# Linear attention and a gated block on one core: unit 0's key exponentials read from the projections' banks, in a new order of operations

## The chip, the core and the metric

The kernel runs on one NeuronCore of a Trainium2 chip. The core's engines work in parallel, each through its own instructions in program order: PE (TensorE, matrix products), DVE (VectorE), ACT (ScalarE, exponentials and copies), POOL (GpSimd) and SP (SyncE, which here only issues transfers). The metric is the device time of one execution in microseconds (us), less is better.

## The reference

Queries, keys and values have 8 batches, 8 heads, 576 tokens and 64 columns. Each of queries and keys is projected onto 128 features, the largest absolute value of a token's projection is subtracted, and the exponential is taken of it and of its negative:

```python
def phi(x):
    proj = np.einsum('bhsd,df->bhsf', x, w_phi)
    proj = proj - np.max(np.abs(proj), axis=-1, keepdims=True)
    return np.concatenate([np.exp(proj), np.exp(-proj)], axis=-1)
q_p, k_p = (phi(q), phi(k))
kv = np.einsum('bhsf,bhsd->bhfd', k_p, v)
z = np.sum(k_p, axis=2)
num = np.einsum('bhsf,bhfd->bhsd', q_p, kv)
den = np.einsum('bhsf,bhf->bhs', q_p, z)[..., None] + 1e-06
```

The quotient num / den, laid out as 4608 tokens of 512 columns, goes through a second block: `h = x @ w_in` (1024 columns), a row's softmax times h, a normalisation over the row, and `@ w_out` back to 512 columns.

## The kernel before

The attention is cut into 16 units (u = 0 to 15) of half a batch, four heads each, and a unit into two subs of two heads. The 576 tokens of a sub's two pairs are taken in groups g = 0, 1, 2 (`GROUPS`): groups 0 and 2 are four tiles of 128 tokens, group 1 is the one tile that the two subs share. The second block has 36 tiles of 128 tokens ("moe", t).

Every piece of work is an `op` with a name, an engine and what it must follow, and the tuple `SEQUENCE`, written out by a search, fixes the order in which the 2458 ops are issued. Each engine runs its own ops in just that order, SP its transfers too. Buffers are rings of slots by tag, handed out in the same order; PSUM has six single banks ("a") and one pair ("h").

The ops that matter here, by name and by the tiles that the profile shows:

- `kp`/`qp` (PE, `pjk`, `pjq`): the projections of a group's keys or queries, both heads of a pair, into two banks, 16 profile records each. `pm` (`pjm`) is that of group 1.
- `km`/`qm` (DVE, `m`): the largest absolute value of each token; `ks`/`qs` (DVE, `dk`, `dq`): projection minus that maximum.
- `ke` (ACT, `ek<-dk`): the exponentials of a key block, first of `dk`, then of its negative, 128x512 each. `qx` (ACT, `fq`) is the same of queries, after a transposition (`dT` on PE for units 0 and 1, through DRAM for the others).
- `K`, `rest`, `Z` (PE, `kvT`): the products with the values and the sums z. For units 3 and up z is added up on POOL first (`zt`, `zacc`). From unit 2 on `kve` (DVE, `kvs`) turns kvT in blocks, `kvo` (SP, `dk<-kvs`) writes it to DRAM and `kvi` (SP, `kvf<-dk`) brings it back as `kvf`.
- `qo`, `qr`, `qd` (PE, `num`, `kvT<-fq,kvf`, `den`): the numerator and the denominator, which read `kvf`. `dv` (POOL, `xa`, `xb`) multiplies by the reciprocal, broadcast back by transfers (`rb`).
- moe `xh`, `xl` (the row block split into two parts, `mxh`, `mxl`), `h` (PE), `mx`, `ex`, `u` (softmax weights), `tb`, `bo`, `bi` (a turn through DRAM, `ub`, `du`, `uTs`), `uh`, `ul`, `o` (PE), `oe` (ACT, `os<-o,sc`) and `od` (SP, `out<-os`). The last tile, 35, is done in two halves of 256 columns (`moe_o_last`).

For units in `K_BANKED` the plan replaces `ks` and `ke` of groups 0 and 2; the tuple is empty before:

```python
if u in K_BANKED:
    add(("kn", g, j), "gpsimd", 250, zj + 0.3, k_neg, (g, j), [("km", g, j)], [("m", ("kn", g, j))], [("m", g, j)])
else:
    add(("ks", g, j), "vector", dve(512), zj + 0.3, k_sub, (g, j), [("km", g, j)], [("d", ("d", g, j))], pj + [("m", g, j)])
```

Of the kernel before, what the change touches and what calls it, by code (L numbers as in the profile page):

```python
# [32 lines left out]
K_BANKED = ()  # L33
# [22 lines left out]
    2, 123, 1, 124, 125, 78, 127, 126, 313, 94, 87, 85, 129, 80, 81, 95, 128, 82, 83, 99, 96, 84, 98, 136, 97,  # L56
    135, 101, 102, 138, 141, 103, 142, 104, 10, 79, 89, 130, 90, 314, 100, 92, 91, 131, 105, 86, 173, 224, 88,
    218, 4, 133, 112, 315, 132, 134, 317, 106, 107, 113, 114, 139, 108, 174, 93, 175, 11, 115, 219, 137, 316,
    110, 12, 178, 116, 109, 111, 117, 143, 222, 189, 181, 180, 182, 33, 140, 5, 118, 154, 13, 179, 318, 220,
    176, 6, 199, 119, 157, 145, 14, 120, 121, 221, 223, 156, 155, 148, 160, 190, 15, 149, 177, 162, 159, 184,  # L60
    28, 38, 150, 284, 22, 275, 122, 158, 161, 197, 34, 200, 183, 198, 191, 194, 192, 187, 193, 7, 195, 201, 225,
    164, 185, 144, 202, 167, 146, 35, 186, 226, 188, 196, 8, 227, 228, 39, 163, 205, 206, 29, 165, 147, 166,
    203, 207, 43, 285, 168, 422, 36, 3, 169, 289, 40, 286, 30, 23, 208, 288, 41, 287, 209, 249, 31, 290, 230,
    204, 213, 214, 232, 233, 236, 231, 255, 44, 381, 252, 210, 268, 151, 372, 235, 215, 234, 296, 24, 229, 291,
    251, 211, 45, 9, 46, 276, 25, 216, 212, 270, 423, 152, 254, 217, 237, 238, 32, 37, 271, 250, 240, 273, 424,
    272, 278, 153, 243, 274, 416, 277, 239, 256, 257, 253, 269, 170, 171, 244, 426, 16, 425, 259, 258, 319, 245,
    241, 42, 292, 262, 48, 49, 365, 246, 172, 279, 297, 50, 325, 427, 263, 260, 449, 242, 294, 382, 47, 264,
    320, 261, 280, 386, 417, 295, 293, 247, 326, 26, 281, 282, 265, 17, 266, 418, 283, 485, 469, 520, 51, 476,
    450, 27, 248, 419, 383, 302, 327, 420, 52, 300, 18, 303, 388, 385, 384, 323, 19, 298, 299, 53, 304, 367,
    321, 301, 267, 368, 305, 421, 369, 387, 308, 20, 21, 1808, 309, 389, 306, 374, 307, 1844, 332, 1826, 334,  # L70
    1809, 521, 72, 322, 324, 486, 329, 60, 328, 1810, 1811, 66, 63, 373, 375, 390, 330, 393, 333, 331, 69, 67,
    522, 345, 428, 370, 310, 371, 593, 336, 394, 61, 524, 1845, 68, 523, 490, 1812, 335, 339, 492, 525, 1813,
    1814, 346, 429, 399, 75, 628, 376, 379, 340, 377, 62, 337, 338, 391, 584, 347, 471, 311, 366, 378, 474, 487,
    73, 1846, 312, 392, 348, 76, 349, 351, 352, 395, 472, 341, 430, 634, 451, 350, 380, 1847, 488, 1817, 491,
    489, 353, 64, 70, 397, 1848, 405, 355, 400, 57, 401, 71, 354, 65, 1827, 54, 1849, 398, 432, 1862, 357, 396,
    55, 532, 1850, 1853, 586, 533, 406, 434, 356, 407, 408, 1828, 1829, 435, 342, 470, 585, 433, 58, 359, 358,
    437, 497, 436, 409, 1854, 475, 410, 1815, 1851, 1830, 74, 431, 473, 493, 455, 498, 594, 629, 411, 439, 438,
    630, 595, 631, 598, 478, 1855, 597, 632, 494, 596, 600, 633, 402, 403, 56, 1831, 404, 412, 360, 599, 413,
    1832, 59, 503, 77, 440, 443, 457, 456, 452, 343, 534, 361, 1818, 1856, 495, 1863, 453, 539, 635, 536, 480,
    362, 363, 414, 496, 1864, 1857, 444, 344, 504, 1852, 477, 1835, 481, 577, 479, 415, 364, 505, 1865, 538,  # L80
    441, 1858, 640, 636, 1866, 483, 482, 1867, 537, 454, 1868, 1859, 509, 459, 1860, 1819, 499, 500, 442, 458,
    637, 638, 484, 1833, 510, 511, 460, 445, 526, 1871, 639, 1820, 698, 579, 512, 461, 540, 501, 506, 1821,
    1816, 535, 446, 690, 541, 462, 463, 502, 464, 580, 447, 705, 1861, 513, 527, 1822, 582, 1872, 1823, 465,
    528, 641, 448, 514, 515, 587, 466, 530, 1869, 529, 1870, 531, 507, 553, 467, 740, 554, 696, 508, 581, 583,
    605, 601, 602, 543, 542, 516, 1824, 606, 544, 611, 588, 468, 545, 517, 665, 1873, 518, 547, 603, 546, 1880,
    604, 741, 742, 697, 555, 589, 548, 744, 556, 1881, 706, 612, 591, 707, 613, 578, 746, 519, 1836, 590, 743,
    1882, 1883, 607, 558, 557, 559, 561, 549, 710, 745, 708, 712, 592, 709, 1884, 560, 562, 700, 566, 666, 703,
    563, 617, 564, 1885, 567, 618, 1886, 565, 569, 568, 619, 642, 817, 689, 550, 1837, 1898, 609, 1934, 610,
    608, 647, 852, 1874, 1935, 1875, 1834, 648, 649, 701, 1936, 620, 1887, 752, 571, 570, 1937, 1876, 1952, 702,
    621, 753, 711, 622, 704, 572, 1938, 1889, 1939, 644, 646, 721, 717, 718, 645, 1899, 1940, 691, 853, 856,  # L90
    650, 643, 614, 1877, 615, 722, 652, 616, 667, 551, 854, 1941, 552, 671, 1900, 1901, 653, 573, 692, 1943,
    1838, 694, 651, 855, 1902, 655, 574, 754, 654, 623, 858, 1878, 1903, 857, 693, 695, 1904, 624, 1953, 1839,
    719, 656, 747, 801, 808, 1890, 575, 668, 657, 713, 714, 625, 669, 803, 659, 748, 658, 1907, 672, 720, 715,
    716, 670, 806, 626, 818, 749, 804, 750, 660, 1825, 802, 627, 822, 819, 674, 821, 1954, 673, 1840, 1888,
    1942, 723, 576, 726, 727, 724, 725, 676, 824, 864, 820, 675, 805, 1841, 661, 1842, 677, 751, 729, 807, 823,
    825, 679, 826, 678, 756, 730, 964, 680, 1891, 731, 732, 827, 681, 683, 759, 761, 1892, 865, 662, 921, 1908,
    699, 663, 757, 810, 929, 733, 760, 859, 1909, 682, 1916, 860, 777, 684, 862, 1905, 965, 861, 758, 1910,
    1893, 1955, 1894, 829, 830, 828, 685, 734, 778, 1895, 920, 735, 686, 767, 762, 1956, 863, 966, 968, 763,
    728, 664, 835, 967, 969, 687, 1944, 809, 755, 1957, 1896, 766, 764, 930, 1958, 769, 812, 765, 1959, 1961,
    889, 815, 1897, 813, 1879, 779, 736, 768, 688, 1988, 780, 783, 2024, 782, 785, 771, 1041, 1843, 737, 1989,  # L100
    1911, 1962, 1026, 1990, 1991, 816, 931, 1960, 2025, 836, 738, 1992, 1993, 1912, 772, 1994, 1997, 814, 890,
    739, 1963, 932, 2006, 781, 1913, 2026, 2027, 841, 784, 934, 1970, 790, 791, 970, 1906, 1082, 1032, 1998,
    770, 773, 866, 774, 811, 831, 786, 1964, 913, 832, 788, 837, 936, 787, 1965, 935, 1914, 1995, 2028, 789,
    933, 842, 2007, 792, 843, 838, 2029, 871, 941, 793, 844, 833, 971, 873, 891, 834, 795, 2030, 868, 794, 915,
    839, 2008, 895, 1945, 2009, 1999, 896, 845, 942, 892, 870, 893, 869, 1966, 796, 840, 916, 976, 972, 2010,
    2033, 974, 918, 917, 973, 2011, 1917, 867, 1971, 1076, 1033, 922, 775, 846, 797, 1915, 874, 1967, 2034, 872,
    776, 924, 876, 919, 923, 798, 977, 878, 879, 847, 975, 2012, 877, 1001, 875, 881, 848, 937, 1968, 938, 927,
    880, 1077, 925, 928, 939, 883, 2000, 894, 940, 897, 947, 1042, 1972, 849, 1080, 1043, 850, 1078, 2001, 1996,
    1079, 945, 884, 2013, 1002, 914, 851, 978, 885, 1003, 2015, 1973, 948, 2002, 1025, 1046, 1045, 898, 900,
    1946, 946, 980, 882, 2003, 953, 1044, 799, 949, 1974, 902, 903, 1047, 1975, 1081, 926, 899, 1048, 901, 800,  # L110
    1947, 954, 955, 904, 1976, 982, 981, 2004, 905, 907, 1979, 1027, 886, 1188, 1083, 956, 2031, 957, 1086, 943,
    887, 906, 2035, 1028, 1088, 908, 983, 944, 985, 1084, 1030, 958, 1144, 1031, 1194, 1153, 888, 979, 1948,
    909, 1007, 1004, 1918, 1949, 1919, 984, 986, 2036, 987, 1029, 1085, 1087, 2005, 1980, 1089, 1034, 1008, 910,
    1950, 911, 991, 950, 951, 988, 1137, 1090, 990, 952, 2032, 1920, 989, 959, 1113, 1005, 1051, 992, 960, 1052,
    993, 1921, 961, 1922, 995, 912, 994, 2096, 1189, 1154, 1049, 1009, 1036, 1155, 1095, 1190, 1925, 1191, 2097,
    1114, 1923, 2078, 1192, 996, 2098, 2037, 1158, 1039, 962, 1147, 1926, 1156, 1159, 2099, 2038, 1053, 963,
    1146, 1969, 1927, 997, 2016, 1300, 1951, 1115, 998, 2039, 2100, 1050, 1165, 1006, 1097, 1010, 1193, 1065,
    1040, 2014, 1157, 1037, 1014, 2101, 1015, 1057, 1160, 1012, 1054, 2017, 2042, 1058, 1091, 1059, 1060, 2040,
# [1188 lines left out]
```

## Time and profile before

| | |
|---|---|
| median of 3 runs | 663.16 us (662.53 to 663.62) |
| the profiled execution's own time | 664.01 us |
| its span, first to last instruction | 662.2 us |
| PE busy | 653.7 us, 99% of the span |
| DVE, ACT, POOL busy | 495.1, 368.9, 409.1 us |
| granted TensorE clock | 1.000 throughout |

The span leaves out 1.81 us that lie around it in the execution's time. "Busy" is the time in which an engine had an instruction in work; consecutive matmuls overlap, so a busy PE need not run at its best pace.

### The profile page before, as it was taken

What the parts mean: (1) busy time and instruction counts of PE and PEld (TensorE: products, weight loads), DVE (VectorE), ACT (ScalarE), POOL (GpSimd) and SP (SyncE); (2) the same over time, 40 slices, a digit from 0 to 9 for tenths busy, and PEclk for the clock granted to TensorE, in tenths of its full rate; (3) what the DMA queues carried; (4) which work ended last, traced back from release to release, by engine and by line L of the source; (5) the groups of instructions that cost most, each with busy time, mean ns of one, the idle gap of its engine ahead of it and who ended that gap; (6) DMA issues with size and microseconds to landing.
All of it is one profiled execution on the core that took longest, in us unless ns stands there. A gap on an engine that the chain in (4) does not pass through costs nothing.

```text
span 662.2 us, 13124 instructions
## 1 busy us (share of the span) xinstructions
PE 653.7 (99%) x4900; PEld 490.5 (74%) x4900; DVE 495.1 (75%) x750; ACT 368.9 (56%) x713; POOL 409.1 (62%) x447
## 2 busy tenths in 40 slices
PE   8999999999999999999999999999999999999997
PEld 6766767668777777777777777877677877788886
DVE  6999987788978687799968879788679665355340
ACT  4997775466564744556565665355745464324221
POOL 0239998757866546667876575856654775455342
PEclk9999999999999999999999999999999999999999
DMA  8987787887487946887667856874786544424241
GB/s 269 346 270 237 221 251 210 270 259 214 134 265 255 296 151 182 272 260 230 201 197 230 287 151 176 266 227 124 229 282 199 191 149 120 123 110 162 112 167 72
DMA packets 133296, 138.45 MB, mean 209 GB/s; under 512 B 55664, under 2 KB 106736, under 8 KB 132720
## 3 DMA queue, kind: packets, MB, share of 16 engines
q1 hardware_dynamic: 133232, 137.61, 65.9%
q8 instruction: 39, 0.64, 0.4%
q14 instruction: 25, 0.20, 0.1%
HBM read 87.10 MB, written 50.48 MB: 208 GB/s over the span
## 4 chain that ended last, share of the span: by engine, by line
PE 87%; DVE 6%; DMA 4%; issue 1%; ACT 1%; SPq 0%; ACTq 0%
PE o L260 30%; PE h L260 29%; PE kvT L260 11%; PE num L260 6%; PE pjk L260 4%; PE pjq L260 4%; PE den L260 2%; DVE m L260 2%; DVE w L260 1%; DVE dq L260 1%; DMA rawq<-in_q 1%; DVE dk L260 1%; DMA pT<-dqd 1%; PE pjm L260 1%; DMA dk<-kvs 1%
## 5 line engine op out<-in xcount | busy, mean ns | idle before, releaser
L260 POOL TENSOR_TENSOR uls<-uTs,uhs 128x1024 fp32r<-128x1024 f32 x36 | 86.6, 2410 | 61.8 <-ACT uhs L260 47.6
L260 PE MATMUL o<-w_out_h,uhs 128*128 128x512 f32 (+1 forms) x296 | 114.6, 387 | 0.0
L260 ACT ACTIVATE ek<-dk 128x512 f32<-128x512 f32 (+1 forms) x160 | 89.7, 584 | 44.1 <-DVE dk L260 39.4
L260 PE MATMUL o<-w_out_l,uhs 128*128 128x512 f32 (+1 forms) x296 | 113.6, 384 | 0.0
L260 PE MATMUL o<-w_out_h,uls 128*128 128x512 f32 (+1 forms) x296 | 113.5, 383 | 0.0
L260 PE MATMUL h<-win_h,mxh 128*128 128x512 f32 x288 | 91.2, 398 | 0.3 <-DVE dq L260 0.3
L260 DVE TENSOR_REDUCE nm<-h 128x1 f32<-128x1024 f32 x36 | 43.9, 1218 | 62.9 <-PE h L260 62.9
L260 PE MATMUL h<-win_l,mxh 128*128 128x512 f32 x288 | 88.9, 390 | 0.0
L260 PE MATMUL h<-win_h,mxl 128*128 128x512 f32 x288 | 88.8, 389 | 0.0
L260 ACT ACTIVATE fq<-pT 128x512 f32<-128x512 f32 (+1 forms) x140 | 74.5, 559 | 21.4 <-DMA pT<-dqd 13.8
L260 POOL TENSOR_TENSOR zt<-ek 128x512 f32<-128x512 f32 x52 | 68.8, 1322 | 24.4 <-ACT ek L260 22.8
L260 ACT ACTIVATE eu<-h,nm 128x1024 f32<-128x1024 f32 x36 | 40.0, 1111 | 69.3 <-DVE nm L260 60.3
L260 PEld LDWEIGHTS o<-w_out_h,uhs 128*128 128x128 f32 x296 | 55.6, 188 | 13.4 <-issue 1.6
L260 PEld LDWEIGHTS o<-w_out_h,uls 128*128 128x128 f32 x296 | 55.6, 188 | 11.0
L260 PEld LDWEIGHTS o<-w_out_l,uhs 128*128 128x128 f32 x296 | 55.6, 188 | 10.6
L260 PEld LDWEIGHTS h<-win_h,mxh 128*128 128x128 f32 x288 | 52.4, 188 | 13.9 <-issue 1.1
L260 PEld LDWEIGHTS h<-win_l,mxh 128*128 128x128 f32 x288 | 54.0, 188 | 11.5
L260 PEld LDWEIGHTS h<-win_h,mxl 128*128 128x128 f32 x288 | 54.1, 188 | 11.5
L260 PE MATMUL kvT<-ek,rawv 128*64 128x256 f32 x512 | 61.9, 384 | 0.0
L260 POOL TENSOR_TENSOR xa<-E,rb 128x576 f32<-128x576 f32 (+1 forms) x32 | 29.7, 931 | 51.9 <-DMA rb<-d 40.7
L260 DVE TENSOR_TENSOR eu<-h,eu 128x1024 f32<-128x1024 f32 x36 | 43.6, 1212 | 17.9 <-ACT eu L260 17.7
L260 PE MATMUL num<-fq,kvf 128*64 128x448 f32 (+1 forms) x304 | 56.2, 500 | 0.0
(96 smaller groups left out, 1231.9 us busy)
## 6 DMA issues: line engine op xcount, KB each, us to landing
du<-ub SPq DMA_DIRECT2D x36, 512.0 KB, 3.7
uTs<-du SPq DMA_DIRECT2D x36, 512.0 KB, 4.9
rb<-d SPq DMA_DIRECT2D x64, 144.0 KB, 4.4
dqd<-dq SPq DMA_DIRECT2D x14, 640.0 KB, 4.3
pT<-dqd SPq DMA_DIRECT2D x14, 640.0 KB, 5.8
out<-os SPq DMA_DIRECT2D x35, 256.0 KB, 3.2
rawq<-in_q SPq DMA_DIRECT2D x32, 256.0 KB, 4.7
rawk<-in_k SPq DMA_DIRECT2D x32, 256.0 KB, 4.5
```

The lines of the kernel that those rows point to most:

```text
L260: return self.tc.keep_in_program_order(method(*args, **kwargs))
```

## The change

Unit 0's eight key exponentials of groups 0 and 2 (two groups, two heads, two signs) no longer read DVE's differences `dk`. ACT reads the projection straight from its PSUM banks, with the maximum as a bias for each token. A bias is one value for each partition, and a 128x512 block holds four tiles of tokens, so that each exponential is issued as four of 128x128. The negative of the maximum is made by POOL (`kn`). The four `ks` of unit 0 go. These functions stood in the kernel unused:

```python
def k_neg(st, g, j):
    st["kn", g, j] = sb("m", [P, 4], name="kn")
    nc.gpsimd.tensor_scalar(out=st["kn", g, j], in0=st["m", g, j], scalar1=-1.0, scalar2=None, op0=ALU.mult)

def k_exp_banks(st, g, j, s, tag):
    if s == 0:
        st["kf", g, j] = sb(tag, [P, 4, 2, F], name="ek")
    for t in range(4):
        nc.scalar.activation(
            out=st["kf", g, j][:, t, s, :], in_=tokens(st["pj", g][j])[:, t], func=AF.Exp, scale=1.0 - 2.0 * s,
            bias=st["m" if s else "kn", g, j][:, t : t + 1],
        )
```

The diff is one line, and a new `SEQUENCE` for the whole program:

```diff
-K_BANKED = ()
+K_BANKED = (0,)
@@
 SEQUENCE = (
-    2, 123, 1, 124, 125, 78, 127, 126, 313, 94, 87, 85, 129, 80, 81, 95, 128, 82, 83, 99, 96, 84, 98, 136, 97,
...
```

The three places that follow show the new order. The first is ACT at the program's start, before; `ek` are key exponentials, `fq` query exponentials, `wraw` the weights' conversion, `kvs` the copy of unit 0's first kvT.

```order
L260 ACT_TABLE_LOAD
L260 ACTIVATE ek<-dk 128x4x128
L260 ACTIVATE fq<-dT 128x512 x2
L260 ACTIVATE ek<-dk 128x4x128
L260 ACTIVATE fq<-dT 128x512
L260 ACTIVATE ek<-dk 128x4x128 x2
L260 ACTIVATE ek<-dk 128x2x128 x2
L260 ACTIVATE fq<-dT 128x512
L260 ACTIVATE ek<-dk 128x4x128
L260 ACTIVATE wraw_234<-wraw_234 128x1024
L260 COPY kvs<-kvT 128x384
```

The same place after the change.

```order
L259 ACT_TABLE_LOAD
L259 ACTIVATE ek<-pjk,kn 128x128 x4
L259 ACTIVATE ek<-pjk,m 128x128 x4
...
L259 ACTIVATE wraw_186<-wraw_186 128x1024
L259 ACTIVATE ek<-dk 128x2x128 x2
L259 ACTIVATE fq<-dT 128x512
L259 ACTIVATE ek<-pjk,kn 128x128 x8
L259 ACTIVATE ek<-pjk,m 128x128 x4
L259 ACTIVATE fq<-dT 128x512
L259 ACTIVATE ek<-pjk,m 128x128 x4
...
L259 COPY kvs<-kvT 128x384
```

The query exponentials that stood among the first key exponentials now stand behind them, the weights' conversion comes earlier, and five key instructions of 128x512 ahead of `kvs` have become 32 of 128x128 (three of group 2 stood behind it).

The second place is PE in the middle of unit 3, before: the sums z of its sub 0 (`kvT<-zacc`), one tile of the second block (`h`), two projections, sub 1's product (`kvT<-ek,rawv`), and then the first product that needs sub 0's `kvf` (`kvT<-fq,kvf`).

```order
L260 MATMUL den<-fq,kvf 32x288 x8
L260 MATMUL kvT<-zacc,ones 32x128 x4
L260 MATMUL h<-win_h,mxh 128x512 x2
...
L260 MATMUL h<-win_h,mxl 128x512 x2
L260 MATMUL pjm<-wph,rawk 128x128 x2
L260 MATMUL pjm<-wph,rawq 128x128 x2
L260 MATMUL pjq<-wph,rawq 128x128 x8
L260 MATMUL kvT<-ek,rawv 64x256 x8
L260 MATMUL kvT<-fq,kvf 64x128 x4
```

The same place after the change.

```order
L259 MATMUL kvT<-zacc,ones 32x128 x4
L259 MATMUL den<-fq,kvf 32x288 x8
L259 MATMUL pjk<-wph,rawk 128x128 x8
L259 MATMUL h<-win_h,mxh 128x512 x2
...
L259 MATMUL h<-win_h,mxl 128x512 x2
L259 MATMUL pjq<-wph,rawq 128x128 x8
L259 MATMUL pjm<-wph,rawk 128x128 x2
L259 MATMUL pjm<-wph,rawq 128x128 x2
L259 MATMUL kvT<-ek,rawv 64x256 x8
L259 MATMUL kvT<-fq,kvf 64x128 x4
```

The denominator of unit 2's sub 1 and one key projection now stand between the sums z and the product that needs `kvf`.

The third place is SP's last transfers, before: `uTs` and `du` are tile 35's turn through DRAM, `out` the results.

```order
L260 DMA du<-ub 128x1024
L260 DMA uTs<-du 128x4x256
L260 DMA out<-os 128x512 x4
L260 DMA out<-os 128x256
L260 DMA out<-os 128x512
L260 DMA out<-os 128x256
L260 DMA out<-os 128x512
```

The same place after the change.

```order
L259 DMA du<-ub 128x1024
L259 DMA out<-os 128x512 x3
L259 DMA uTs<-du 128x4x256
L259 DMA out<-os 128x512 x5
L259 DMA out<-os 128x256 x2
```

The program now ends with the two halves of tile 35; before, a whole tile (33) came last.

## Rows read from the trace of the kernel before

**Rows 1.** The page: PE's busy time, and the chain that ended last by engine.

```profile
PE 653.7 (99%) x4900; PEld 490.5 (74%) x4900; DVE 495.1 (75%) x750; ACT 368.9 (56%) x713; POOL 409.1 (62%) x447
PE 87%; DVE 6%; DMA 4%; issue 1%; ACT 1%; SPq 0%; ACTq 0%
```

**Rows 2.** Busy time by stretch: PE, weight loads, DVE, ACT, POOL; clock, DMA share, GB/s.

```profile
0.00:13.00 13.00, 10.40 (x112) 9.29 (x112) 7.76 (x17) 5.23 (x10) 1.26 (x12) 1.00 0.81 267
13.00:35.00 22.00, 21.80 (x291) 14.89 (x290) 21.93 (x41) 19.55 (x37) 4.80 (x2) 1.00 0.99 340
35.00:67.00 32.00, 31.47 (x452) 21.96 (x452) 31.90 (x55) 27.38 (x55) 21.20 (x14) 1.00 0.80 245
67.00:105.00 38.00, 36.60 (x312) 25.40 (x312) 33.88 (x57) 26.61 (x59) 37.14 (x34) 1.00 0.80 246
105.00:560.00 455.00, 455.00 (x3274) 338.73 (x3271) 362.05 (x538) 260.50 (x511) 300.42 (x332) 1.00 0.69 215
```

**Rows 3.** PE's waits, whole span: us in total, times, longest.

```profile
PE kvT L260 <- DMA kvf<-dk: 1.3, 1, 1.3
PE pjk L260 <- DMA rawk<-in_k: 0.8, 1, 0.8
PE h L260 <- DVE dq L260: 0.3, 1, 0.3
```

**Rows 4.** Timeline of the first 13 us: start, length, engine, instruction, idle before.

```profile
5.13 1.29 DVE L260 TENSOR_REDUCE m<-pjq 128x4 f32<-128x512 f32 x2 [5.13 <-PE pjq L260]
7.13 0.69 DVE L260 TENSOR_REDUCE m<-pjk 128x4 f32<-128x512 f32 x1
8.34 0.68 DVE L260 TENSOR_TENSOR dk<-pjk,m 128x512 f32<-128x512 f32 x1
9.05 0.63 ACT L260 ACTIVATE ek<-dk 128x512 f32<-128x512 f32 x1 [7.05 <-DVE dk L260]
...
10.64 0.63 ACT L260 ACTIVATE ek<-dk 128x512 f32<-128x512 f32 x1
10.98 2.06 PE L260 MATMUL pjq<-wph,rawq 64*128 64x128 f32 x32 [0.25 <-PE pjk L260]
11.16 0.60 ACT L260 ACTIVATE fq<-dT 128x512 f32<-128x512 f32 x1
12.96 1.95 PE L260 MATMUL kvT<-ek,rawv 128*64 128x256 f32 x16
```

**Rows 5.** Small instructions: two groups (count, busy us, mean ns), then two timeline rows.

```profile
L260 ACT COPY E<-kvT 128x128 f32<-128x128 f32 x26 | 6.7, 260 | 1.3 <-DVE kvs L260 1.3
L260 POOL TENSOR_SCALAR sa<-sm 128x1 f32<-128x1 f32 x36 | 8.8, 245 | 6.3 <-ACT eu L260 3.5
650.07 1.26 ACT L260 ACTIVATE os<-o,sc 128x512 f32<-128x512 f32 x2 [4.33 <-PE o L260]
652.93 0.47 ACT L260 ACTIVATE os<-o,sc 128x256 f32<-128x256 f32 x1 [1.60 <-issue]
```

**Rows 6.** The chain that ended last, near 90 us: start, length, what.

```profile
89.54 0.59 DVE kvs L260
...
90.15 5.31 DMA dk<-kvs
...
95.48 4.27 DMA kvf<-dk
...
102.31 0.97 PE den L260 x16
```

**Rows 7.** The end: ACT's and SP's last rows; the results' transfers, us to landing.

```profile
658.56 0.69 ACT L260 ACTIVATE os<-o,sc 128x512 f32<-128x512 f32 x1 [2.32 <-PE o L260]
659.27 0.33 SPq L260 DMA_DIRECT2D out<-os  x1
DMA to landing us min/median/max: 1.7/2.4/3.2
out<-os SPq DMA_DIRECT2D x2, 128.0 KB, 1.7
```

254 rows, old and new, of the table SEQUENCE are left out of this document.

## The prediction

> **What bounds the kernel now.** I read the page first. PE is busy 99% of the span, and 87% of the chain that ended last is PE's own work [rows 1]. So the question is not which engine is the slowest but where PE still waits, and what lies after its last product. The windows by stretch answer the first half: from 105 to 560 us PE is busy 455.00 of 455.00 us, and nothing can be won there; it falls short by 2.60 us up to 13 us, by 0.20 and 0.53 us in the next two stretches and by 1.40 us from 67 to 105 us [rows 2]. The list of PE's waits names the largest single one: 1.3 us, once, for the transfer that brings `kvf` back; 0.8 us falls on the first key load and 0.3 us on DVE ahead of the first `h` [rows 3]. A reader should also see what stands close behind PE. From 13 to 67 us DVE is busy 53.83 of 54 us, ACT has 2.45 us free up to 35 us and 4.62 us up to 67, and from 67 to 105 us POOL is busy 37.14 of 38 us [rows 2]. In the first 100 us four engines are nearly full, and an order can gain or lose by a few us; later it can only lose.
>
> **What the change removes and adds, in the first 67 us.** Four `ks` of unit 0 leave DVE. Consecutive 512-wide pieces there start (8.34 - 7.13) / 2 = 0.605 us apart [rows 4], so 2.4 us go. The new order puts the first key maximum ahead of the first `dq`: DVE ends the query maxima at 5.13 + 1.29 = 6.42 us and then stands until the keys' projection is there, at 7.13 [rows 4], where the old order worked. That costs 0.7 us, and DVE is 1.7 us ahead from there on.
>
> POOL makes four small negatives. The nearest row is its one-column tensor-scalar of 0.245 us [rows 5]; four are 1.0 us, and POOL is all but idle up to 35 us [rows 2], so only their latency counts, 0.25 us ahead of ACT's first use.
>
> ACT pays. Eight exponentials of 512 columns, which start 0.52 us apart (10.64 to 11.16 [rows 4]), 4.2 us in all, become 32 of 128 columns that read PSUM and take a per-partition bias. No row is such an instruction. The nearest is the copy of `o`, which reads PSUM with a per-partition scale: 0.69 us for 512 columns, 0.47 for 256, two of 512 in 1.26 [rows 5, 7]. A column is then (0.69 - 0.47) / 256 = 0.86 ns, an instruction of 128 columns 0.36 us long, and neighbours overlap by 2 x 0.69 - 1.26 = 0.12 us, which leaves 0.24 us from start to start. The upper bound is 0.36 (no overlap), the lower 0.260 - 0.12 = 0.14 us, from the 128-wide copy without an operand for each partition [rows 5]. I take 0.25, by the row that has both the PSUM source and the operand. ACT then has 32 x 0.25 = 8.0 us in place of 4.2: 3.8 us more.
>
> The Trainium skill, "ScalarE: Activation LUTs", section "What ACT_TABLE_LOAD costs", speaks against such a split: it gives an ACTIVATE with a pointer operand about 280 ns and 0.833 ns a column, with 93 ns of overlap between neighbours. By it a 128-wide one would be an estimated 0.29 us from start to start, and the 32 of them 9.4 us, 5.2 us more than now; no run so far shows this instruction.
>
> Where the surplus goes: ACT can start once the first maximum (7.13 + 0.69) is negated, at about 8.1 us in place of 9.05 [rows 4], which takes 0.95 us of it; the 2.45 us free up to 35 us and a part of the 4.62 after take the rest. By 67 us it is absorbed. On the way, the pair "h" that holds the first keys comes free only when the sixteenth small exponential has read it, at 8.1 + 16 x 0.25 = 12.1 us; unit 0's second query projection waits for that pair and takes 0.99 us (half of 12.96 - 10.98 [rows 4]), and `K` follows at 13.1 us against 12.96. I charge 0.3 us for it, since the query transpositions ahead now wait for later DVE pieces too. At 0.36 us a piece it is 8.1 + 5.8 + 1.0 = 14.9, 1.9 us later; at 0.14 us DVE's pieces end last and nothing is lost. In the other direction PE has 0.73 us of waits between 13 and 67 us [rows 2], and 0.3 of them are for DVE [rows 3]; DVE is ahead by 1.7 us, so I credit 0.5. The early part is 0.3 - 0.5 = -0.2 us, with 1.9 us above and 1.7 us (all of DVE's lead) below.
>
> **The middle: one wait is covered.** Behind the sums z of unit 3's sub 0 the chain is DVE's turn (0.59 us), the way out (5.31) and the way back (4.27) [rows 6]: 10.2 us with nothing to spare, and PE's work between was 1.3 us too short [rows 3]. The new order moves a denominator (0.97 us [rows 6]) and a key projection (0.99) into that gap: 1.96 us more cover against 1.3 us of wait. I take -1.3 us; the other bound is 0, if something else ends as late.
>
> From 105 us on, PE keeps every product and changes its tile shape between neighbours about as often (164 places against 167); I charge nothing.
>
> **The end.** Before, the last piece is a whole tile: 0.69 us on ACT, then a 256 KB transfer issued at 659.27 us, 2.93 us before the span ends. After, the last is half of tile 35: 0.47 us on ACT and 128 KB, which landed in 1.7 us; the eight last transfers had a median of 2.4 [rows 5, 7]. PE's work is the same and tile 35 now has eight half tiles of cover where it had seven. The copy gives 0.22 us, the transfer between 0 and 2.93 - 1.7 = 1.2 us; I take 0.4, near half the step from 2.4 to 1.7. Together -0.6 us.
>
> **Sum.** -0.2 - 1.3 - 0.6 = -2.1 us on the profiled execution's own time of 664.01 us (span 662.2, 1.81 us around it): 661.9 us. That execution lies 0.85 us above the median of 663.16 us, so the median goes to 661.1 us, 0.3% less. About 0.2%, 1.3 us, is what a measurement of this kernel tells from no change.
>
> **Rivals.**
>
> *The covered wait comes back on POOL.* In the new order POOL divides unit 2's first result (`xa`, `xb`) ahead of the last piece of unit 3's sub-1 sums; before it came behind. The division waits for `rb`, whose transfer SP issues behind the very `kvf` transfer above, and `Z` of sub 1 waits for the sums. POOL has 0.86 us to spare in that stretch [rows 2]. If this wait is as long as the old one, -1.3 falls away: 662.4 us. Against it: PE's piece `h` and more lie between.
>
> *ACT holds PE up in the first 45 us.* This one ends slower. At 0.36 us a piece the surplus is 32 x 0.36 - 4.2 = 7.3 us, and 0.95 + 2.45 us of room by 35 us leave 3.9 us that everything behind it on ACT (query exponentials, `kvs`, `kvf` copies, weights) comes late; the first `h` would follow 3.5 us late, and the sum is +3.5 - 1.3 - 0.6 = +1.6: 664.8 us. It decides from about 0.30 us a piece, where the pair "h" comes free at 12.9 us, the time at which `K` starts now.
>
> *DVE's lead reaches PE whole.* DVE has no idle time up to 67 us and the first `h` waits for it, which speaks for it; that PE itself has only 0.73 us of waits there speaks against it. -1.7 - 1.3 - 0.6: 659.5 us.
>
> *The order adds small waits later.* Between 105 and 560 us PE now has none, so every one made there counts in full; with 2 us of them the change comes out at 663.1 us, no change.
>
> **How the numbers follow.** The forecast 0.40, POOL's wait 0.25, ACT late 0.15, DVE's lead 0.15, late waits 0.05. Faster by over 0.2% are the forecast and DVE's lead, with a little of POOL's: 0.57. Within 0.2% are most of POOL's and the late waits: 0.28. Slower is ACT's: 0.15. The range from 659.4 to 663.8 us takes in the DVE case and POOL's with the unknown price of an exponential up to some 0.32 us, and leaves out ACT at its worst. The forecast's own range is 660.3 to 661.8.
>
> **What would show it.** In the profile after: 32 exponentials `ek<-pjk` of 128x128 with starts 0.25 us apart, ACT's first at 8.1 us, `K` of unit 0 near 13.2 us; no wait of the first `h` for DVE; no wait of PE for `kvf<-dk`; a 0.47 us ACT piece and a 128 KB transfer at the end, the piece starting 3.0 us before the span ends where it was 3.64. Wrong would make it: exponentials 0.30 us apart or more; a PE wait on `zacc` near 100 us; waits of PE past 105 us.

## The result: 0.7% slower, and the profile after

The changed kernel takes 667.69 us at the median of 4 runs (666.85 to 670.02), against 663.34 us (662.53 to 663.62) for the kernel before: a ratio of 1.0073, 95% interval 1.0046 to 1.0101. I had forecast 661.1 us. The profiled execution is the longest of the four (670.02 us, span 668.2), so a second profile of the same kernel stands among the experiments, and a wait is taken as the kernel's own where both show it. L259, L260 and L253 in the rows are one helper's line in files of different length.

First the page of the kernel after, for [rows 1]: PE's share is 98% in place of 99, and only the chain's parts tell where to look.

```profile
PE 657.0 (98%) x4900; PEld 492.9 (74%) x4900; DVE 492.6 (74%) x746; ACT 371.1 (56%) x737; POOL 407.6 (61%) x451
PE 88%; DMA 4%; DVE 3%; ACT 3%; POOL 1%; issue 1%; SPq 1%; POOLq 0%; DVEq 0%; ACTq 0%
```

The windows by stretch, columns as in [rows 2], with the second stretch cut at 19 us:

```profile
0.00:13.00 13.00, 10.04 (x94) 8.57 (x94) 7.60 (x17) 4.30 (x14) 1.72 (x14) 1.00 0.81 260
13.00:19.00 6.00, 4.72 (x36) 3.26 (x40) 3.91 (x8) 6.00 (x21) 0.41 (x2) 0.72 1.00 334
19.00:35.00 16.00, 16.00 (x246) 11.67 (x245) 14.44 (x27) 14.98 (x33) 4.78 (x2) 1.00 0.83 271
35.00:67.00 32.00, 32.00 (x462) 22.55 (x460) 30.82 (x50) 28.59 (x57) 18.18 (x13) 1.00 0.82 261
67.00:105.00 38.00, 36.69 (x303) 25.27 (x302) 33.42 (x56) 27.04 (x58) 35.77 (x33) 1.00 0.81 250
105.00:560.00 455.00, 452.39 (x3282) 335.73 (x3273) 357.97 (x537) 255.57 (x506) 293.33 (x323) 1.00 0.69 213
```

Two stretches are new. From 13 to 19 us PE is idle for 1.28 us, at a granted clock of 0.72 (a mean of stretches at 2.4 and at 1.2 GHz); before, the clock was 1.00 there. And from 105 to 560 us, where PE had been busy to the last hundredth, 2.61 us are missing. PE's waits name the places, for [rows 3]:

```profile
PE pjq L259 <- ACT ek L259: 2.3, 1, 2.3
PE cmall L259 <- DVE kvs L259: 1.3, 1, 1.3
PE kvT L259 <- DVE dk L259: 1.1, 1, 1.1
PE den L259 <- DVE qz L259: 0.9, 1, 0.9
```

The wait for `kvf` is gone, the first `h` no longer waits for `dq`, and these four stand in their place (shorter ones, and those before the first projections are done, are left out). The timeline of the start, for [rows 4], shows the first:

```profile
6.69 0.69 DVE L259 TENSOR_REDUCE m<-pjk 128x4 f32<-128x512 f32 x1
7.57 0.23 POOL L259 TENSOR_SCALAR kn<-m 128x4 f32<-128x4 f32 x1 [5.58 <-DVE m L259]
7.90 0.68 DVE L259 TENSOR_REDUCE m<-pjk 128x4 f32<-128x512 f32 x1
8.68 1.28 ACT L259 ACT_TABLE_LOAD   x1 [8.68 <-DVE m L259]
9.98 1.14 ACT L259 ACTIVATE ek<-pjk,kn 128x128 f32<-128x128 f32 x4
10.99 1.16 ACT L259 ACTIVATE ek<-pjk,m 128x128 f32<-128x128 f32 x4
12.00 1.20 ACT L259 ACTIVATE ek<-pjk,kn 128x128 f32<-128x128 f32 x4
13.00 1.23 ACT L259 ACTIVATE ek<-pjk,m 128x128 f32<-128x128 f32 x4
14.28 1.99 PE L259 MATMUL pjq<-wph,rawq 64*128 64x128 f32 x16 [2.28 <-ACT ek L259]
16.20 2.73 PE L259 MATMUL kvT<-ek,rawv 128*64 128x256 f32 x16
```

The small exponentials start (13.00 - 9.98) / 12 = 0.252 us apart. They begin late: the negative of the first maximum is there at 7.80 us, but ACT waits for the second maximum, which ends at 8.58, and only then loads its activation table, 1.28 us. Before, that load was over at 2 us:

```profile
0.72 1.28 ACT L260 ACT_TABLE_LOAD   x1 [0.72 <-PEq L1297]
```

The instructions' list tells why: the first exponential depends on PE, DVE and POOL, and two of the three waits stand ahead of the table load. The wait on DVE is for its fifth instruction, the second key maximum; the one on PE is for the first key projection, long done.

```
1 L259 ACT_TABLE_LOAD [waits DVE_49,PE_49]
2 L259 ACTIVATE ek<-pjk,kn 128x128 [waits Pool_49]
```

The old first exponential waits for DVE alone, so its load waits for nothing. The Trainium skill, "Perfetto Trace Analysis", section "Identifying Dependency Chains", says that an instruction which waits for several engines may get instructions with the further waits inserted ahead of it; the list agrees, and the row at 8.68 us shows that here they stand ahead of the table load too.

The second place is near 375 us. The rows show DVE, POOL and PE (`qz` is DVE's product for the denominator, from unit 4's sub 1 on; most take 0.8 us).

```profile
375.34 4.11 DVE L259 SCALAR_TENSOR_TENSOR qz<-fq,kvf,qz 128x576 f32<-128x576 f32 x1
379.38 0.68 DVE L259 TENSOR_TENSOR dk<-pjk,m 128x512 f32<-128x512 f32 x1
...
375.25 1.27 POOL L259 TENSOR_TENSOR zacc<-zacc,ek 64x512 f32<-64x512 f32 x1
376.49 2.35 POOL L259 TENSOR_TENSOR uls<-uTs,uhs 128x1024 fp32r<-128x1024 f32 x1
...
378.45 0.65 PE L259 MATMUL kvT<-ek,vz 64*64 64x256 f32 x4
380.20 0.65 PE L259 MATMUL kvT<-ek,vz 64*64 64x256 f32 x4 [1.10 <-DVE dk L259]
380.80 1.08 PE L259 MATMUL den<-qz,ones 128*32 128x288 f32 x5
...
382.57 0.73 PE L259 MATMUL h<-win_h,mxh 128*128 128x512 f32 x2 [0.23 <-DVE eu L259]
```

The product ends 0.6 us behind POOL's second instruction and spans both. The difference `dk` behind it frees a bank that PE's `rest` needs, the next product feeds `den`, and `eu` behind that frees the pair for `h`: PE is late three times over. The wait of `den` in the list above is another one, near 352 us, where two more products took 2.66 us beside an instruction of POOL.

At the end, for [rows 7]: the last piece on ACT starts 668.2 - 665.17 = 3.03 us before the span ends, where it was 3.64.

```profile
665.17 0.47 ACT L259 ACTIVATE os<-o,sc 128x256 f32<-128x256 f32 x1 [2.35 <-PE o L259]
```

### The profile page after: what moved, and what is told of

Same layout as the page of the kernel before. It is cut to its first block, busy times and chain, and to the rows that moved or that the text cites. A ratio compares the mean times of both kernels' runs of the same rounds, so it can differ in the third digit from the quotient of the medians.

```text
span 668.2 us, 13162 instructions
## 1 busy us (share of the span) xinstructions
PE 657.0 (98%) x4900; PEld 492.9 (74%) x4900; DVE 492.6 (74%) x746; ACT 371.1 (56%) x737; POOL 407.6 (61%) x451
## 4 chain that ended last, share of the span: by engine, by line
PE 88%; DMA 4%; DVE 3%; ACT 3%; POOL 1%; issue 1%; SPq 1%; POOLq 0%; DVEq 0%; ACTq 0%
PE o L259 29%; PE h L259 28%; PE kvT L259 12%; PE num L259 6%; PE pjk L259 4%; PE pjq L259 4%; PE den L259 3%; DMA dk<-kvs 1%; DVE qz L259 1%; DMA dqd<-dq 1%; PE pjm L259 1%; ACT ek L259 1%; POOL wsum L259 1%; DVE dq L259 1%; DMA rb<-d 1%
## 5 line engine op out<-in xcount | busy, mean ns | idle before, releaser
L259 PE MATMUL o<-w_out_h,uhs 128*128 128x512 f32 (+1 forms) x296 | 114.3, 386 | 0.0
L259 POOL TENSOR_TENSOR uls<-uTs,uhs 128x1024 fp32r<-128x1024 f32 x36 | 87.0, 2416 | 43.9 <-ACT uhs L259 33.8
L259 PE MATMUL o<-w_out_l,uhs 128*128 128x512 f32 (+1 forms) x296 | 113.6, 384 | 0.0
L259 PE MATMUL o<-w_out_h,uls 128*128 128x512 f32 (+1 forms) x296 | 113.5, 383 | 0.0
L259 ACT ACTIVATE ek<-dk 128x512 f32<-128x512 f32 (+1 forms) x152 | 84.1, 591 | 39.5 <-DVE dk L259 32.0
L259 DVE TENSOR_REDUCE nm<-h 128x1 f32<-128x1024 f32 x36 | 43.8, 1218 | 69.8 <-PE h L259 69.8
L259 PE MATMUL h<-win_h,mxh 128*128 128x512 f32 x288 | 91.8, 400 | 0.4 <-DVE eu L259 0.4
L259 PE MATMUL h<-win_l,mxh 128*128 128x512 f32 x288 | 89.0, 390 | 0.0
L259 PE MATMUL h<-win_h,mxl 128*128 128x512 f32 x288 | 88.8, 390 | 0.0
L259 ACT ACTIVATE fq<-pT 128x512 f32<-128x512 f32 (+1 forms) x140 | 74.0, 560 | 25.4 <-PE kvT L259 13.0
L259 ACT ACTIVATE eu<-h,nm 128x1024 f32<-128x1024 f32 x36 | 40.0, 1111 | 70.5 <-DVE nm L259 60.3
L259 POOL TENSOR_TENSOR zt<-ek 128x512 f32<-128x512 f32 x52 | 67.7, 1301 | 16.8 <-ACT ek L259 15.9
L259 PEld LDWEIGHTS o<-w_out_h,uhs 128*128 128x128 f32 x296 | 55.6, 188 | 12.8 <-issue 1.4
L259 PEld LDWEIGHTS o<-w_out_h,uls 128*128 128x128 f32 x296 | 55.6, 188 | 11.0
L259 PEld LDWEIGHTS o<-w_out_l,uhs 128*128 128x128 f32 x296 | 55.7, 188 | 10.7
L259 PEld LDWEIGHTS h<-win_h,mxh 128*128 128x128 f32 x288 | 52.2, 188 | 14.8 <-issue 2.3
L259 PEld LDWEIGHTS h<-win_l,mxh 128*128 128x128 f32 x288 | 54.1, 188 | 11.6
L259 PEld LDWEIGHTS h<-win_h,mxl 128*128 128x128 f32 x288 | 54.0, 188 | 11.7 <-POOL mxl L259 0.2
L259 PE MATMUL kvT<-ek,rawv 128*64 128x256 f32 x512 | 62.5, 387 | 0.0
L259 PE MATMUL num<-fq,kvf 128*64 128x448 f32 (+1 forms) x304 | 55.8, 500 | 0.0
L259 DVE SCALAR_TENSOR_TENSOR qz<-fq,kvf,qz 128x576 f32<-128x576 f32 x46 | 47.3, 1049 | 11.4 <-ACT qz L259 11.3
L259 ACT ACTIVATE qz<-fq,kvf 128x576 f32<-128x576 f32 x46 | 34.7, 771 | 36.3 <-DMA kvf<-dk 36.2
```

The costliest lines, as they stand in the source:

```text
L259: return self.tc.keep_in_program_order(method(*args, **kwargs))
```

## The experiments

The theories: **A**, the start is late because the table load stands behind the first wait; **B**, the price of the small exponentials; **C**, the new order as such; **D**, products `qz` that stand still while POOL works.

### The table loaded early (e1_early)

```diff
+    pad = const.tile([P, 96], F32, name="pad")
...
     zero = tc.nc.const_aps.tensor(0.0, [P, P], F32)
+    nc.scalar.activation(out=pad[:, :1], in_=zero[:, :1], func=AF.Exp)
```

> The changed kernel with one exponential of one column, of a constant zero, put first on ACT, so that the load of the activation table has nothing to wait for. Theory A (the table load is what starts late): the load runs near 1 us instead of 8.68; the first small exponential starts at 8.7 us instead of 9.98, since it still waits for the second key maximum, which ends at 8.58; the pair "h" comes free at 12.9 instead of 14.2, unit 0's K starts near 14.9 instead of 16.2. 1.3 us off the time if only the wait shrinks; up to 2.9 us if the shorter idle time of PE also leaves the granted clock of 13 to 19 us at 1.00 (it is 0.72 after the change): 664.8 to 666.4 us. Rival B (the price or the number of the small exponentials is what costs): the sixteen still end 4.0 us after the first, and the time moves by 1.3 us at most. Rival C (late waits at 282, 351 and 378 us make up the loss, the start is absorbed by 105 us): no change, 667.7 us.

666.28 us at the median, ratio to the kernel before 1.0039 (1.0025 to 1.0053). Its timeline:

```profile
0.72 1.28 ACT L259 ACT_TABLE_LOAD   x1 [0.72 <-PEq L1297]
...
8.84 1.14 ACT L259 ACTIVATE ek<-pjk,kn 128x128 f32<-128x128 f32 x4 [6.62 <-DVE m L259]
...
13.14 1.16 PE L259 MATMUL pjq<-wph,rawq 64*128 64x128 f32 x16 [1.00 <-ACT ek L259]
14.23 1.95 PE L259 MATMUL kvT<-ek,rawv 128*64 128x256 f32 x16
```

As A has it: the exponentials come 1.14 us sooner, PE's wait is 1.00 in place of 2.28 us, the granted clock from 13 to 19 us is 1.00, and `K` starts 1.97 us earlier. In the time are 1.4 us against the first run of the changed kernel and 2.0 us against its second (below). Both are more than the 1.3 us that B allows, the first by less than the noise, and the sixteen still end 4.0 us after the first. The rest of the loss is elsewhere.

### The new order with the old differences (e2_neworder_ks)

```diff
-K_BANKED = (0,)
+K_BANKED = ()
```

> The new order with K_BANKED empty: DVE makes the four differences again and ACT eight exponentials of 128x512. Theory A (the start's loss comes from the exponentials taken from the banks, with the table load behind the first wait): K of unit 0 back near 13 us, granted clock of 13 to 19 us at 1.00, and the late waits near 282, 351 and 378 us stay, since they belong to the order: 663.5 to 665.0 us, that is 2.7 to 4.2 us less than the changed kernel. Rival C (all of the loss belongs to the order): 667 us or more, with DVE 2.4 us busier in the first 67 us.

668.13 us, 1.0069 (1.0055 to 1.0084): as slow as the change, which is C's number where I had expected A's. The table is loaded at 0.72 us here, but the exponentials now wait for DVE, whose first maxima and query work stand ahead of the differences, and PE's clock falls as well:

```profile
0.00:13.00 13.00, 9.82 (x91) 8.65 (x92) 7.44 (x16) 4.11 (x6) 1.27 (x12) 0.93 0.82 270
13.00:19.00 6.00, 6.00 (x40) 4.03 (x43) 6.00 (x11) 4.39 (x10) 0.00 (x0) 0.58 0.91 264
```

The wait `kvT <- DVE dk` of 1.1 us stands in its trace too. With the table early in both, taking the exponentials from the banks was worth 668.13 - 666.28 = 1.85 us in this order; with the table late, as the change has it, they are worth nothing (668.25 in the second run below). So in this order the loss is there without the exponentials from the banks too; at the start it comes by another wait.

### Three products moved (e3_late_fix)

```diff
 SEQUENCE, by operation, DVE's part:
+(10, vg, 0, 1), (10, vg, 0, 0)
 (moe, 15, var)
-(10, vg, 0, 1), (10, vg, 0, 0)
...
+(10, vg, 1, 0)
 (moe, 14, mx)
...
-(10, vg, 1, 0)
```

> The changed kernel with three products qz of unit 10 moved earlier among DVE's instructions: two to ahead of the statistics (var) of tile 15, one to ahead of the maximum of tile 14, into 1.8 us in which DVE is idle. Theory D (DVE's products qz, which read two SBUF operands, stand still while POOL works: 4.11 us for one at 375.34 us, where most take 0.8): the waits of PE at 351 (0.94 us) and 378 (1.10 us and what follows, 1.9 us by PE's starts) go, and the time falls by 2 to 3 us, to 664.7 to 665.7 us; the start stays as it is. Rival E (the waits are there because everything on DVE is late since the start): they move to the next place and the time stays within 0.7 us of 667.7.

667.35 us, 1.0057 (1.0045 to 1.0069): the size that E gives, but not for E's reason. The moved product ran free, and the one left behind met the same two instructions of POOL (from 374.37 to 377.96 us here):

```profile
369.40 0.81 DVE L253 SCALAR_TENSOR_TENSOR qz<-fq,kvf,qz 128x576 f32<-128x576 f32 x1
...
375.05 3.52 DVE L253 SCALAR_TENSOR_TENSOR qz<-fq,kvf,qz 128x576 f32<-128x576 f32 x1
```

D stands, and the edit was half of what it needs.

### The old order with the new exponentials (e4_oldorder_kn)

```diff
-K_BANKED = ()
+K_BANKED = (0,)
 SEQUENCE, the old one; each moved to just ahead of the operation that needs its bank:
+(0, ke, 0, 1, 1), (0, qx, 0, 0, 1), (2, qs, 0, 0), (0, ke, 2, 0, 1), (0, ke, 2, 1, 1)
```

> The old order with K_BANKED = (0,): unit 0's exponentials are taken from the banks, in the old sequence but for five exponentials or differences of the first 75 operations that come earlier because their banks are needed. Theory A: the table load again starts behind the first key maxima, near 9 us, K of unit 0 starts at 16 us or later, and no wait of PE past 105 us: 665.5 to 667.5 us. Rival C (the loss belongs to the new order): within 1 us of the kernel before, 662.5 to 664.5 us.

672.04 us, 1.0136 (1.0121 to 1.0151): A's side, but more than twice its size. ACT's table load starts at 9.31 us, query exponentials stand among the sixteen, and PE waits for the pair longer than anywhere else. From 105 us on PE's list has no wait, so the late ones came with the new order.

```profile
PE pjq L253 <- ACT ek L253: 5.5, 1, 5.5
```

### The changed kernel again (e5_control)

> The changed kernel once more, beside the runs that follow. Its first profiled execution was 2.3 us above its median, so a second look shows which of its waits are always there. Every theory: 667 to 668 us. If products qz of DVE are held up by POOL in every execution, one of 4.1 us stands near 375 us again and PE's waits of about 1.9 and 0.9 us by its starts follow near 378 to 382 us; the waits near 282 and 351 us may differ.

668.25 us (666.81 to 668.82), 1.0066 (1.0052 to 1.0079). The second profile, span 665.8 us, shows the waits for the pair (2.3), for `dk` (1.1) and of `cmall` (0.8); the one of `den` near 352 us is not there.

```profile
15.78 3.59 PE L259 MATMUL kvT<-ek,rawv 128*64 128x256 f32 x16
...
69.50 0.97 PE L259 MATMUL h<-win_h,mxh 128*128 128x512 f32 x2
...
372.88 4.13 DVE L259 SCALAR_TENSOR_TENSOR qz<-fq,kvf,qz 128x576 f32<-128x576 f32 x1
```

The first two rows are for the next run. The same product took 4.11 us once and 4.13 us four times in the five profiles that leave it in place in the new order (two of this kernel, e1, e2 and e6).

### PE kept busy in its wait (e6_filler)

```diff
+        for _ in range(4 if (st["u"], sub, j) == (0, 0, 1) else 1):
             for t, d in enumerate(parts):
                 nc.tensor.transpose(out=pt[:, t * P : (t + 1) * P], in_=d, identity=ident)
```

> The changed kernel in which PE does the second query transposition of unit 0 four times over, with the same result, in the 2.3 us in which it waits for the pair "h". Theory F (the low granted clock of 13 to 19 us, 0.72, follows PE's idle time there, and costs 1.7 us by 19 us): the clock stays at 1.00, the projection behind the wait takes 1.0 us in place of 2.0 and K 1.9 in place of 2.7, and the time falls by 0.5 to 1.7 us. Rival G (the clock falls because PE had little work in the first 13 us, or the 1.7 us are absorbed behind it, since PE waits for others up to 105 us): the time stays within 0.5 us of the control.

667.69 us (665.65 to 671.59), 1.0066 (1.0042 to 1.009). The clock is as F wants it: `K` starts at 15.81 us, beside 15.78 in the control, and takes 1.95 in place of 3.59 us.

```profile
13.00:19.00 6.00, 5.04 (x75) 3.48 (x77) 4.73 (x8) 6.00 (x21) 0.41 (x2) 1.00 0.97 308
...
14.72 1.16 PE L259 MATMUL pjq<-wph,rawq 64*128 64x128 f32 x16 [0.96 <-ACT ek L259]
15.81 1.95 PE L259 MATMUL kvT<-ek,rawv 128*64 128x256 f32 x16
...
67.20 0.99 PE L259 MATMUL h<-win_h,mxh 128*128 128x512 f32 x2
```

The medians differ by 0.56 us, between what F and G had forecast, and with intervals of up to 1.6 us to either side they cannot decide. The rows say more. PE is 1.6 us ahead of the control behind `K` and 2.3 us at the first `h` (67.20 against 69.50), since the wait for `cmall` is gone too; it is still 2.3 us ahead at 282 us. About 1 us of that goes near 283 us, where a key projection waits for a bank that ACT's output copy frees, and about 1 us near 350 us, at a product `qz` that POOL holds up: PE's wait there is 0.7 us in this profile and absent in the control's. The changed kernel's first profile also loses time at both places. So G's second half, that the gain is absorbed by 105 us, does not hold in these two profiles; how much of it reaches the end changes with the execution, and the medians leave it open. By the first `h` e1_early is no further (67.41 us): up to there the low clock can account for all that the late table load costs.

### Early table and all four products (e7_early_late2)

```diff
+    nc.scalar.activation(out=pad[:, :1], in_=zero[:, :1], func=AF.Exp)
 SEQUENCE: as in e3_late_fix, and
+(10, sg, 1, 0, 1), (10, vg, 1, 0), (10, vg, 1, 1)
 (moe, 14, mx)
```

> The changed kernel with the early load of the activation table, with unit 10's two products qz of sub 0 ahead of the statistics of tile 15, and now with both of sub 1 (and the scaling on ACT that feeds the second) ahead of the maximum of tile 14: in the run with only one of them moved, the other met POOL's work and took 3.5 us. Theory D: both take about 0.8 us near 370 us, PE's waits near 375 us go, and the time falls by 2 us or more below that of the early load alone (666.3): 663.7 to 664.6 us. Rival E (the waits move on to the next place): 666 us.

663.25 us, 0.9992 (0.9981 to 1.0003): the loss is gone, as D says. The group of all 46 products (ns: least, median, most), first of the changed kernel's first profile, then of this one:

```profile
L259 DVE SCALAR_TENSOR_TENSOR qz<-fq,kvf,qz x46: 767/815/4106, 151.9 to 563.9; 128x576 f32<-128x576 f32 x46
```

```profile
L253 DVE SCALAR_TENSOR_TENSOR qz<-fq,kvf,qz x46: 766/812/1995, 148.0 to 555.6; 128x576 f32<-128x576 f32 x46
```

PE there goes from `rest` to `den` to `h` without a wait:

```profile
372.82 0.66 PE L253 MATMUL kvT<-ek,vz 64*64 64x256 f32 x8
...
374.26 0.73 PE L253 MATMUL h<-win_h,mxh 128*128 128x512 f32 x2
```

From `rest` to `h` are 1.44 us, where the changed kernel took 382.57 - 378.45 = 4.12. A long product by itself need not cost PE anything: the kernel before has one of 2.73 us and e9_late2 one of 3.05, and neither profile lists a wait of PE behind 105 us. What counts is what follows on DVE.

### Two edits in the old order (e8_oldfix)

```diff
 SEQUENCE, the old one:
+(3, Z, 0)
 (2, qd, 1)
-(3, Z, 0)
...
+(moe, 33, o, 1)
 (moe, 35, o, 0), (moe, 35, o, 1)
...
-(moe, 33, o, 1)
```

Tile 33's statistics and scale move up with it, and its result goes out ahead of tile 35's; tile 32's output copy also comes earlier, since it frees a slot.

> The old order with two edits that the new one makes: the sums z of unit 3's sub 0 ahead of the denominator of unit 2's sub 1, so that the way of kvf through DRAM starts 0.97 us sooner, and the two halves of tile 35 last. If my terms for the middle and the end were right, -0.97 and -0.6 us: 661.9 us, faster than the kernel before by 0.2%. If the wait for kvf comes back elsewhere, only the end is won: 662.9 us.

662.81 us, 0.9991 (0.9981 to 1.0000), 0.58 us below the kernel before beside it, at the edge of the noise. The end alone would give that: the last piece starts 660.3 - 657.22 = 3.08 us before the span ends, as after the change. The run makes both edits at once, so it does not separate the two terms, but nothing is left for the 0.97 us of the middle.

```profile
657.22 0.47 ACT L253 ACTIVATE os<-o,sc 128x256 f32<-128x256 f32 x1 [2.40 <-PE o L253]
```

### The products alone (e9_late2)

The edit is that of e7_early_late2 without its first line.

> The changed kernel with the four products qz of unit 10 moved as in the run before that had both edits, but with the activation table loaded where the change puts it. If the two causes add up, this is the control (668.25) less what the products cost. By the runs with the early load (666.28 and 663.25) that is 3.0 us: 665.2 us, PE's wait of 2.3 us for the pair "h" still there, no wait near 375 us. If they do not add up (a late start shifts the products into POOL's work), 666.5 us or more.

665.17 us, 1.0030 (1.0021 to 1.0040). The two causes add up. Early table: 668.25 - 666.28 = 1.97 us alone, 665.17 - 663.25 = 1.92 with the products moved. Products: 668.25 - 665.17 = 3.08, and 666.28 - 663.25 = 3.03.

### The old differences, products moved (e10_ks_late2)

```diff
-K_BANKED = (0,)
+K_BANKED = ()
 SEQUENCE: as in e9_late2
```

> The new order with the four products qz moved and K_BANKED empty: DVE's differences are back, the table load is early because the first exponential waits for one engine. Against the kernel with both edits and the exponentials from the banks (663.25) it tells what taking them from the banks is worth in this order. If it is worth what it was without the moves (668.13 - 666.28 = 1.85 us): 665.1 us. If it is worth nothing: 663.3 us.

663.90 us, 1.0009 (0.9998 to 1.0019): between the two forecasts. Against e7 the exponentials from the banks, with the table early, would be worth 0.65 us here; the two intervals overlap, so that it is not shown.

### The kernel before again (e11_before)

> The kernel before once more, for a second profile. If PE's wait of 1.3 us for kvf near 98 us is always there, it shows again; the kernel with the two edits of the old order lost it and gained only 0.6 us at the median, so a shorter wait is expected, of 0.2 to 0.6 us, or none. 663.4 us.

663.07 us, 0.9993 (0.9984 to 1.0001): no difference, as it must be. PE's second profile has no wait for `kvf`:

```profile
99.17 0.61 PE L260 MATMUL kvT<-fq,kvf 128*64 128x128 f32 x8
...
91.00 0.33 SPq L260 DMA_DIRECT2D dk<-kvs  x1
...
93.81 0.60 SPq L260 DMA_DIRECT2D kvf<-dk  x1
```

The 1.3 us of [rows 3] were one execution's. PE lost 1.0 us at the start here, on `dT <- DVE dq`, and came to the place 0.85 us later, but the way out to DRAM began 0.85 us later too (91.00 against 90.15 [rows 6]), so that this is not the reason. The way out was shorter: 93.81 - 91.00 = 2.81 us to the way back, where it had been 5.31 [rows 6]. The median of the 28 such transfers, from issue to landing, is 2.4 us in the first profile and 2.3 in this one.

### A version that beats both (e12_best)

```diff
+    nc.scalar.activation(out=pad[:, :1], in_=zero[:, :1], func=AF.Exp)
 SEQUENCE: as in e9_late2, and
+(0, km, 0, 1)
 (0, qs, 0, 0)
...
-(0, km, 0, 1)
```

> The changed kernel with the early table load, the four products qz moved, and DVE's two first key maxima one behind the other, ahead of the two query differences. The first small exponential waits for the second maximum, so it should start near 8.2 us in place of 8.84, the pair "h" come free at 12.2 in place of 12.9, and the second query projection start 0.7 us earlier: 662.5 us, 0.1% to 0.2% below the kernel before. If the query differences, 0.6 us later, hold PE up instead (its key projection of group 2 waits for their banks), 663.2 us.

661.70 us, 0.9978 (0.9968 to 0.9987): faster than the kernel before by 0.2%.

```profile
8.30 1.14 ACT L253 ACTIVATE ek<-pjk,kn 128x128 f32<-128x128 f32 x4 [6.09 <-PE pjq L253]
...
12.61 1.16 PE L253 MATMUL pjq<-wph,rawq 64*128 64x128 f32 x16 [0.40 <-ACT ek L253]
13.70 1.95 PE L253 MATMUL kvT<-ek,rawv 128*64 128x256 f32 x16
```

ACT starts 0.54 us sooner than in e7 (its row names PE's projection, which ends at 8.19 us, as last; the maximum that it waits for ends at 8.18), `K` is at 13.70 us, and the query differences that come later hold nothing up that shows. The median falls by 1.55 us against e7, more than the 0.7 expected. PE's rows are ahead of e7's by 0.53 us at `K` and by 0.95 at `cmall`, whose wait is gone, and this lead is lost near 281 us, at a wait of 0.4 us for a bank. But e7's profiled execution was the fastest of its eleven (661.81 us) and this one was not (662.24), so the rest of the 1.55 us cannot be read from the two.

## Why the prediction was wrong

**The price was right.** 0.25 us for an exponential of 128 columns: measured 0.252. POOL's negative: 0.225 us in its group's mean, taken as 0.245. By the rival of a late ACT the change turns slower from 0.30 us a piece; it turned slower at 0.252. The estimate of 0.29 us, worked out from the Trainium skill, "ScalarE: Activation LUTs", section "What ACT_TABLE_LOAD costs", is above the measured value.

**The early part: the step that failed is that ACT can start once the first maximum is negated, at about 8.1 us.** It started at 9.98. 1.28 us is the table load behind the first waits, which e1 against e5 and e7 against e9 show to be worth 1.9 to 2.0 us of the time, the fall of PE's clock that follows included; the rest is the second maximum, for which the first exponential waits too, and moving that maximum up goes with a further 1.55 us (e12). The pair came free at 14.2 us in place of 12.1, and `K` started at 16.20 in place of 13.1. The sum also has no term for PE's clock: in the two profiles it was 0.72 and 0.73 from 13 to 19 us, and `K` took 2.73 and 3.59 us in place of 1.95. Behind 19 us the credit for DVE's lead did come: PE's 0.73 us of waits up to 67 us are gone, and in e12 too, where PE is not late. It was lost again on `cmall`, which the new order puts right ahead of the first `h`: 1.3 and 0.8 us in the two profiles, nothing in e12.

**The step that charges nothing from 105 us on failed too, and it cost more than the table load.** I compared what PE computes and looked at no engine that feeds it. The products `qz` cost 3.0 to 3.1 us (e7 and e9 against e1 and e5). By PE's rows (4.12 - 1.44) = 2.7 us of them are near 380 us. The late waits that I gave a chance of 0.05 are this. The rule is in the Trainium skill, "SBUF — State Buffer", section "Who interferes with whom": a DVE instruction with two inputs in SBUF shares a read interface with a GpSimd instruction that reads SBUF, and whichever starts first shuts the other out. The trace agrees, 4.11 us against 0.8, and the product spans two of POOL's instructions in a row.

**The middle, -1.3 us, was read from one slow transfer.** "Nothing to spare" took 5.31 us for the way out as what it always takes; in the kernel's second profile it is 2.81 us and PE does not wait (e11). e8, which shortens this path in the old order, won no more than the end's share. My range for this term ended at 0, which is about where it belongs.

**The end was right.** -0.6 us forecast; the stretch from the last ACT piece to the end shrank from 3.64 to 3.03 us, and e8, which makes this edit with another, won 0.58.

Summed: 1.95 (table) + 3.05 (products) + 1.55 (second maximum and what went with it) = 6.55 us are what the three edits took off the control's 668.25, and 661.70 is left, 1.8 us below the kernel before beside it (663.54). I had forecast 2.1 less. Of the 1.8 us, 0.6 is the end and perhaps 0.65 the banked exponentials, which their intervals do not show; some 0.5 us I cannot place.

**Rivals.** POOL's wait near 100 us did not come. ACT did hold PE up, at the place I named and for another reason. DVE's lead could not reach PE whole, since PE had no more than 0.73 us of waits to lose there.

## What to carry to other kernels

Before an instruction is made an engine's first, see which engines it waits for: a table load that hid behind the first transfers comes onto the path when its own instruction waits for several. When an order changes, look at pairs of DVE instructions with two SBUF inputs and POOL instructions that now run side by side, far from the edit too: here one such pair cost more than the whole edit could win. And a wait of PE that one execution shows should be seen in a second before it is charged, or at least set beside its group: 5.31 us for a transfer whose median was 2.4 stood in the first trace.

## What the runs showed of the hardware that was not expected

A product of 128x576 on DVE took 4.13 us in profile after profile where 0.8 is usual, to within 0.02 us, behind two instructions of POOL.

The granted clock of 13 to 19 us was 0.72 with a wait of PE of 2.28 us just before, 1.00 with waits of 1.05 and 1.00 us (e1), and 0.58 with no wait above 0.82 us (e2), so the longest wait alone does not tell it. `K` took 3.59 us in the control, where part of the stretch is at 1.2 GHz, and 1.95 at 2.4 GHz (e6). The 2.3 us that PE was ahead by the first `h` lasted to 282 us and were then mostly lost at two places where some executions of one kernel lose time and others do not, so that one profile beside another does not price a cause.

A transfer of 192 KB to DRAM took 5.31 us from its issue to the next one in one execution of the kernel before and 2.81 us in another.
